# Two mixture-of-experts layers behind a random-feature attention: batch 0's sums of squares on ScalarE and VectorE, omega's low part from PSUM, late constants behind a maximum, gate matrices side by side

## The chip, the core and the metric

The kernel runs on one core of a Trainium2 chip. The engines are TensorE (PE, with its weight loads PEld), VectorE (DVE), ScalarE (ACT), GpSimd (POOL) and SyncE (SP, which issues most transfers). Each engine works through its own queue in order and waits at an instruction until what it needs is there. The metric is the device time of one execution in microseconds; a kernel is run several times and the median counts.

## What is computed

The reference is a chain of three steps on 2 batches of 576 tokens, 8 heads of 64.

```python
def phi(x):                                   # x: q or k, scaled by 64**-0.25
    h = einsum('bhsd,md->bhsm', x, omega)     # omega: 128 x 64
    h = h - sum(x * x, axis=-1) / 2
    return exp(h - max(h)) / sqrt(128)
kv, z = einsum(k_p, v), sum(k_p)              # per head, over all tokens
attn = (q_p @ kv) / (q_p . z + 1e-6)          # 1152 x 512 after the heads are joined

logits = attn @ w_gate                        # 8 experts, top 1 of a token
y = p(top1) * sigmoid(attn @ w_output_gate)[top1] * relu(attn @ w1[e]) @ w2[e]

out = sum over 4 experts of probs[:, e] * relu(y @ dw1[e]) @ dw2[e]
```

All in float32. The kernel writes each operand of a large product as a high part (rounded to the float32r format) and a low part (the rest), and takes high x high, high x low and low x high.

## The kernel before

The attention goes first and takes about the first 130 us. A group is one batch and half of the heads (four): `(b, hh)`. A group has 4 x 128 tokens of its own; the 64 tokens left over of both batches are kept together as `kr`, `vr`, `qr` (called the rest). The loop at the end of `moe_stack`'s attention part runs over `banks`, in the order k of a group, then q of it: 4 banks each (two token blocks `jp`, two head pairs `hp`), plus one bank of the rest for each half of the heads in batch 0. For a bank the steps are:

- `squares`, once for a group's k or q and for the rest: sum over 64 of x*x into `sq`, which the bias of the exponential needs. Before the change the first group's k goes on VectorE (a product and a reduction for each of its four transfers) and the eight others on GpSimd, as one product and six halving additions.
- `stage_a`: four transposes on PE into a PSUM tile `pt`, then the scaled copy `qTh` on ScalarE and the low part `qTl` on VectorE.
- `stage_b`: three products per half bank with omega's high part `omh` and low part `oml` into `pj`; on VectorE the maximum `mx`, then two small instructions with `sq` that give the bias `nb`; on ScalarE four exponentials `e`.
- `stage_ck` (k) adds to `kv` in PSUM; `stage_cq` (q) transposes `e`; `stage_d` multiplies with `kvs`, divides on VectorE, transposes and writes the high part `xh` (ScalarE) and the low part `xl` (VectorE) of the attention's output.

When a batch is through, `gate` takes the gate logits (`gate_logits`, `gate_tr`), and `main_expert` finds the expert that most tokens of the batch chose; SP reads its number and loads its weights. The products of the first expert layer (`ph`) are already mixed into batch 1's attention. Behind that come the layers of the two mixtures, which take the other 500 us.

What an engine does next is set by the order in which a scheduler in the compiler laid out the instructions; the queues hold that order at run time. `prep_late` makes constants that the gates need (`fold`, `cmask`, `iota` and others, and the high and low parts of the gate matrices) and the second mixture's probabilities `pb`. It is called at step `LATE`, but the scheduler may move its instructions up to where their inputs are there. Omega's high part is copied out of a float32 copy `omT`, its low part is `omT` less `omh`. The `WARM` products `wu` at the start use only constants.

Of the kernel before, what the change touches and what calls it, by code (L numbers as in the profile page):

```python
# [9 lines left out]
F32 = mybir.dt.float32  # L10
F32R = mybir.dt.float32r
# [10 lines left out]
M = 128  # L22
# [2 lines left out]
KB, FB = DM // 128, FF // 128  # L25
NC = 288
NX = B * S
WARM = 8
LATE = 12
HBUFS = 4  # L30
GROUPS = ((0, 320), (640, 256))
# [7 lines left out]
def moe_stack(ctx, tc, q, k, v, omega, w_gate, w_ogate, mw1, mw2, dprobs, dw1, dw2, out):  # L39
# [3 lines left out]
    def f32(ap):  # L43
        return ap.bitcast(F32)
# [34 lines left out]
    rev = cp.tile([128, NE], F32, name="rev")  # L79
    ue = cp.tile([128, 4, NE], F32, name="ue")  # L80
    uc = cp.tile([128, 4, NE], F32, name="uc")
    lgr = cp.tile([16, 128], F32, name="lgr")
    cnt = cp.tile([128, 4, NE], F32, name="cnt")
    ohb = cp.tile([128, 2, NE], F32, name="ohb")
    pb = cp.tile([128, 9, NE2], F32, name="pb")
# [88 lines left out]
        nc.sync.dma_start(dpr[64 * b:64 * b + 64, 8, :], dprobs[S * b + 512:S * b + 576])  # L174


    omT = cp.tile([128, 2, M], F32, name="omT")
    nc.vector.memset(omT, 0.0)
    pt = ps_t.tile([128, 4, 128], F32, tag="pt", name="pt")
    nc.tensor.transpose(pt[:, 0, :], om2.rearrange("p r d -> p (r d)"), ident)  # L180
    for r in range(2):
        nc.scalar.copy(omT[64 * r:64 * r + 64, r, :], pt[64 * r:64 * r + 64, 0, :])
    omh = cp.tile([128, 2, M], F32R, name="omh")
    oml = cp.tile([128, 2, M], F32R, name="oml")
    nc.scalar.copy(omh, omT)
    TT(oml, omT, f32(omh), op=ALU.subtract)
    wgh = cp.tile([128, KB, 16], F32R, name="wgh")
    wgl = cp.tile([128, KB, 16], F32R, name="wgl")

    def prep_late():  # L190
        TT(fold, ident[:, 0:32], ident[:, 32:64], op=ALU.add)
        TT(fold, fold, ident[:, 64:96], op=ALU.add)
        TT(fold, fold, ident[:, 96:128], op=ALU.add)
        nc.vector.tensor_reduce(cmask, ident.rearrange("p (c r) -> p c r", r=32), axis=AX.X, op=ALU.add)
        nc.gpsimd.iota(i32, pattern=[[1, 32]], base=0, channel_multiplier=0)
        nc.vector.tensor_copy(iota, i32)
        TS(iota1, iota, 1.0, None, op0=ALU.add)
        TS(rev, iota[:, 0:NE], -1.0, float(NE), op0=ALU.mult, op1=ALU.add)
        nc.vector.tensor_copy(ue, iota[:, 0:NE].unsqueeze(1).to_broadcast([128, 4, NE]))
        nc.vector.tensor_copy(uc, iota[:, 0:4].unsqueeze(2).to_broadcast([128, 4, NE]))  # L200
        nc.vector.memset(lgr, 0.0)
        split(wgh, wgl, wg)
        ds_ = cp.tile([128, 9], F32, name="ds_")
        nc.vector.tensor_reduce(ds_, dpr, axis=AX.X, op=ALU.add)
        TS(ds_, ds_, 1e-9, None, op0=ALU.add)
        nc.vector.reciprocal(ds_, ds_)
        TT(pb, dpr, ds_.unsqueeze(2).to_broadcast([128, 9, NE2]), op=ALU.mult)
# [3 lines left out]
    def squares(kind, b, hh, eng):  # L211

        src = raw[kind, b, hh] if b < 2 else raw[kind, 2]
        x = src.rearrange("p h j d -> p (h j) d") if b < 2 else src
        n = x.shape[1]
        x2 = ap.tile([128, n, D], F32, tag="x2", name="x2")
        s = ap.tile([128, n], F32, tag="sq" + kind + ("r" if b == 2 else ""), name="sq")
        if eng is nc.vector:
            for h in range(0, n, 4):
                TT(x2[:, h:h + 4], x[:, h:h + 4], x[:, h:h + 4], op=ALU.mult)  # L220
                nc.vector.tensor_reduce(s[:, h:h + 4], x2[:, h:h + 4], axis=AX.X, op=ALU.add)
        else:
            nc.gpsimd.tensor_tensor(x2, x, x, op=ALU.mult)
            w = D // 2
            while w:
                dst = x2[:, :, 0:w] if w > 1 else s.unsqueeze(2)
                nc.gpsimd.tensor_tensor(dst, x2[:, :, 0:w], x2[:, :, w:2 * w], op=ALU.add)  # L227
                w //= 2
        sq[kind, b, hh] = s

    def stage_a(kind, b, hh, jp):

        rest = b == 2
        src = raw[kind, b, hh] if not rest else raw[kind, 2]
        n = 2 if rest else G
        ps = ps_t.tile([128, G, 128], F32, tag="pt", name="pt")
        t, tl = (ap.tile([128, G, 128], F32R, tag=g, name=g) for g in ("qTh", "qTl"))
        for i in range(n):
            blk = src[:, i, 2 * jp:2 * jp + 2, :] if not rest else src[:, G * hh + 2 * i:G * hh + 2 * i + 2, :]
            nc.tensor.transpose(ps[:, i, :], blk.rearrange("p a d -> p (a d)"), ident)  # L240
        nc.scalar.activation(t[:, :n], ps[:, :n], AF.Copy, scale=SCALE)
        STT(tl[:, :n], ps[:, :n], SCALE, f32(t[:, :n]), op0=ALU.mult, op1=ALU.subtract)
        st_a[kind, b, hh, jp] = t, tl

    flip = [0]

    def stage_b(kind, b, hh, jp, hp):

        rest = b == 2
        t, tl = st_a[kind, b, hh, jp]  # L250
        if rest:
            s = sq[kind, 2, 0][:, G * hh:G * hh + G].rearrange("p (a c) -> p a c", a=2)
        else:
            s = sq[kind, b, hh].rearrange("p (h j) -> p h j", j=4)[:, 2 * hp:2 * hp + 2, 2 * jp:2 * jp + 2]
        e = ap.tile([128, 2, 2, M], F32, tag="e" if not rest else f"er{kind}{hh}", name="e", bufs=EB if not rest else 1)
        ps = ps_j.tile([128, 2, 2, M], F32, tag="pj", name="pj")
        for i in range(2):
            x = 2 * hp + i
            nc.tensor.matmul(ps[:, i], t[:, x], omh, start=True, stop=False)
            nc.tensor.matmul(ps[:, i], t[:, x], oml, start=False, stop=False)  # L260
            nc.tensor.matmul(ps[:, i], tl[:, x], omh, start=False, stop=True)
        mx = ap.tile([128, 2, 2], F32, tag="mx", name="mx", bufs=4)
        nc.vector.tensor_reduce(mx, ps, axis=AX.X, op=ALU.max)

        nb = ap.tile([128, 2, 2], F32, tag="nb", name="nb", bufs=4)
        hs = SCALE * SCALE / 2
        STT(mx, s, -hs, mx, op0=ALU.mult, op1=ALU.add)
        STT(nb, s, -hs, mx, op0=ALU.mult, op1=ALU.subtract)
        flip[0] += 1
        if flip[0] % FLIP:  # L270
# [88 lines left out]


    def gate_logits(b, psp, tag):
        lgs = cp.tile([16, 4, 128], F32, tag="lgs", name="lgs")
        for c in range(2):
            ps = psp.tile([16, NC], F32, tag=tag, name="lgp")
            cc = 2 * b + c
            mms = []
            for kb in range(KB):
                for a, x in ((wgh, xh), (wgh, xl), (wgl, xh)):
                    mms.append((a[:, kb, :], x[:, kb, NC * cc:NC * cc + NC]))
            for i, (a, x) in enumerate(mms):  # L370
                nc.tensor.matmul(ps, a, x, start=i == 0, stop=i == len(mms) - 1)
            nc.scalar.copy(lgs[:, 2 * c:2 * c + 2, :], ps[:, 0:256].rearrange("p (t n) -> p t n", n=128))
            nc.vector.tensor_copy(lgr[:, 32 * cc:32 * cc + 32], ps[:, 256:NC])
        return lgs

    def gate_tr(b, lgs, psp, tag):
        ps = psp.tile([128, 5, 16], F32, tag=tag, name="lgt")
        for t in range(5):
            nc.tensor.transpose(ps[:, t, :], lgs[:, t, :] if t < 4 else lgr, ident[:16, :16])
        lg = cp.tile([128, 5, 16], F32, tag=f"lg{b}", name="lg")  # L380
        nc.vector.tensor_copy(lg, ps)
        return lg
# [130 lines left out]
    for st in range(n + LAGD + 2):  # L513
        if st < n:
            kind, b, hh, jp, hp = banks[st]
            if b < 2 and jp == 0 and hp == 0:
                squares(kind, b, hh, nc.vector if (kind, b, hh) == ("k", 0, 0) else nc.gpsimd)
                if kind == "k" and (b, hh) != (0, 0):
                    i = 2 * b + hh + 1
                    if i < 4:  # L520
                        load_group(i // 2, i % 2)
            if b == 2 and hh == 0:
                squares(kind, 2, 0, nc.gpsimd)
            if st == LATE:
                prep_late()
            if hp == 0:
                stage_a(kind, b, hh, jp)
        if 1 <= st <= n:
            stage_b(*banks[st - 1])
        if 0 <= st - 1 - LAG < n:  # L530
            for u in tiles_of(banks[st - 1 - LAG]):
                do_c(u)
        if 0 <= st - 1 - LAGD < n:
            for u in tiles_of(banks[st - 1 - LAGD]):
                do_d(u)
# [389 lines left out]
```

## Time and profile before

| | |
|---|---|
| time of 3 runs | 638.55, 641.35, 645.41 us; median 641.35 |
| the profiled execution | 640.9 us, span 638.5 us, granted clock 0.997 |
| busy in the span | PE 614.5 us (96%), DVE 437.9 (69%), ACT 263.2 (41%), POOL 265.3 (42%) |
| the chain of waits that ended last | PE 84%, DVE 8%, POOL 3% of the span |

Busy time of PE is not PE at its peak: a product that lies in the queue behind another is counted from its start, so that a full stretch reads 100% and a slower one may read 90%. The count of products in a stretch says more. A wait inside an instruction (for a port, say) shows as a longer instruction, not as idle time.

### The profile page before, as it was taken

How to read it: one execution, taken by the hardware profiler on the slowest of the kernel's cores; microseconds unless marked ns; L12 is line 12 of the kernel's file. 1: busy time of each engine (PE TensorE's matmuls, PEld its weight loads, DVE VectorE, ACT ScalarE, POOL GpSimd, SP SyncE). 2: the span in 40 equal slices, each digit the busy share in tenths (PEclk: the TensorE clock that was granted, in tenths of full speed). 3: DMA queues.
4: the chain of work that ended last, by engine and by line, in shares of the span. 5: the costliest groups of instructions: out<-in, count | busy, mean ns of one | idle time of the engine just before them, and what ended most of it. 6: DMA issues, size and time to landing. Idle time of an engine off the chain costs nothing.

```text
span 638.5 us, 10737 instructions
## 1 busy us (share of the span) xinstructions
PE 614.5 (96%) x3985; PEld 564.1 (88%) x3986; DVE 437.9 (69%) x947; ACT 263.2 (41%) x630; POOL 265.3 (42%) x303
## 2 busy tenths in 40 slices
PE   7899999989998999899999999999999999999997
PEld 6788898889998999689989899899899898898995
DVE  6898588885284568976766756756666667666564
ACT  4658575504062234534434433433433343343230
POOL 3994024700000001557537536646646645745220
PEclk9999999989999999999999999999999999999999
DMA  8621034005133302201201201102201102100004
GB/s 200 154 67 34 2 133 132 2 4 195 67 131 133 132 2 67 66 2 37 97 1 59 73 1 67 68 0 67 67 1 66 67 1 67 66 1 2 0 1 148
DMA packets 38180, 39.60 MB, mean 62 GB/s; under 512 B 14448, under 2 KB 26736, under 8 KB 38128
## 3 DMA queue, kind: packets, MB, share of 16 engines
q1 hardware_dynamic: 37840, 38.85, 19.5%
q8 instruction: 31, 0.51, 0.3%
q14 instruction: 21, 0.17, 0.1%
q10 hardware_dynamic: 288, 0.07, 0.0%
HBM read 36.55 MB, written 2.36 MB: 61 GB/s over the span
## 4 chain that ended last, share of the span: by engine, by line
PE 84%; DVE 8%; POOL 3%; issue 1%; SPq 1%; DMA 1%; ACT 1%; POOLq 0%; ACTq 0%
PE po L553 10%; PE po L552 10%; PE po L554 10%; PE pp L552 9%; PE pp L554 9%; PE pp L553 9%; PE py L552 3%; PE py L554 3%; PE py L553 3%; PE ph L553 3%; PE ph L552 3%; PE ph L554 3%; PE pnd L337 2%; POOL x L227 2%; PE kv L289 2%
## 5 line engine op out<-in xcount | busy, mean ns | idle before, releaser
L90 POOL TENSOR_TENSOR wlo<-st,whi 128x512 fp32r<-128x512 f32 x104 | 126.4, 1238 | 241.5 <-ACT whi L89 241.5
L89 ACT CAST whi<-st 128x512 fp32r<-128x512 f32 x144 | 81.8, 596 | 141.4 <-PE po L554 51.9
L874 DVE SCALAR_TENSOR_TENSOR oacc<-po,pb,oacc 128x512 f32<-128x512 f32 x135 | 100.1, 749 | 56.0 <-PE po L554 56.0
L554 PE MATMUL po<-whi,hl 128*128 128x512 f32 x288 | 112.1, 390 | 0.7 <-POOL hl L548 0.6
L552 PE MATMUL po<-whi,hh 128*128 128x512 f32 x288 | 112.5, 391 | 0.0
L553 PE MATMUL po<-wlo,hh 128*128 128x512 f32 x288 | 112.4, 390 | 0.0
L548 POOL TENSOR_TENSOR hl<-c,hh 128x320 fp32r<-128x320 f32 (+1 forms) x64 | 53.2, 831 | 89.1 <-ACT hh L547 76.5
L552 PE MATMUL pp<-xh,whi 128*128 128x320 f32 (+1 forms) x256 | 75.8, 297 | 0.4 <-DVE u L833 0.2
L554 PE MATMUL pp<-xh,wlo 128*128 128x320 f32 (+1 forms) x256 | 75.7, 296 | 0.0
L553 PE MATMUL pp<-xl,whi 128*128 128x320 f32 (+1 forms) x256 | 75.7, 296 | 0.0
L554 PEld LDWEIGHTS po<-whi,hl 128*128 128x128 f32 x288 | 54.0, 188 | 12.9 <-POOL hl L548 1.0
L552 PEld LDWEIGHTS po<-whi,hh 128*128 128x128 f32 x288 | 54.1, 188 | 10.6 <-ACT hh L542 0.2
L553 PEld LDWEIGHTS po<-wlo,hh 128*128 128x128 f32 x288 | 54.1, 188 | 10.0
L821 DVE TENSOR_TENSOR c<-u,pp 128x320 f32<-128x320 f32 (+1 forms) x96 | 43.2, 453 | 21.7 <-PE pp L554 21.2
L546 ACT ACTIVATE c<-c 128x320 f32<-128x320 f32 (+1 forms) x64 | 28.5, 445 | 54.4 <-DVE c L821 53.7
L552 PEld LDWEIGHTS pp<-xh,whi 128*128 128x128 f32 x256 | 48.4, 190 | 2.3 <-DVE u L839 0.6
L553 PEld LDWEIGHTS pp<-xl,whi 128*128 128x128 f32 x256 | 48.5, 190 | 1.2
L552 PE MATMUL ph<-xh,whi 128*128 128x288 f32 (+1 forms) x160 | 47.9, 299 | 1.7 <-issue 1.7
L552 PE MATMUL py<-hh,whi 128*128 128x288 f32 x160 | 49.1, 307 | 0.0
L554 PEld LDWEIGHTS pp<-xh,wlo 128*128 128x128 f32 x256 | 48.5, 190 | 0.0
L553 PE MATMUL ph<-xl,whi 128*128 128x288 f32 (+1 forms) x160 | 48.0, 300 | 0.0
L543 DVE SCALAR_TENSOR_TENSOR hl<-c,hh 128x320 fp32r<-128x320 f32 (+1 forms) x64 | 45.9, 751 | 3.0 <-ACT hh L542 3.0
(217 smaller groups left out, 1424.5 us busy)
## 6 DMA issues: line engine op xcount, KB each, us to landing
st<-in_moe_w_dram SPq DMA_DIRECT2D x32, 512.0 KB, 4.1
st<-in_moe_w_dram SPq DMA_DIRECT2D x12, 1024.0 KB, 5.4
v<-in_v_dram SPq DMA_DIRECT2D x16, 128.0 KB, 3.9
q<-in_q_dram SPq DMA_DIRECT2D x4, 512.0 KB, 5.2
out_dram<-oacc SPq DMA_DIRECT2D x8, 256.0 KB, 2.1
k<-in_k_dram SPq DMA_DIRECT2D x3, 512.0 KB, 5.1
k<-in_k_dram SPq DMA_DIRECT2D x4, 128.0 KB, 2.7
kr<-in_k_dram SPq DMA_DIRECT2D x2, 128.0 KB, 3.6
```

The source lines that it names most:

```text
L89: nc.scalar.copy(hi, src)
L90: eng.tensor_tensor(lo, src, f32(hi), op=ALU.subtract)
L227: nc.gpsimd.tensor_tensor(dst, x2[:, :, 0:w], x2[:, :, w:2 * w], op=ALU.add)
L289: nc.tensor.matmul(kvps[key][:, i, :], e[i][r0:r1], v65[i], start=first and i == 0, stop=last and i == G - 1)
L543: STT(hl, src, 0.0, f32(hh), op0=ALU.max, op1=ALU.subtract)
L546: nc.scalar.activation(c, c, AF.Relu)
L548: nc.gpsimd.tensor_tensor(hl, c, f32(hh), op=ALU.subtract)
L552: nc.tensor.matmul(ps, sh_, mh, start=start, stop=False)
L553: nc.tensor.matmul(ps, sh_, ml, start=False, stop=False)
L554: nc.tensor.matmul(ps, sl_, mh, start=False, stop=stop)
L821: TT(c, u, p, op=op)
L874: STT(oacc[:, T], po, pc, oacc[:, T], op0=ALU.mult, op1=ALU.add)
```

## The change

`squares` with `nc.vector` now takes the products on ScalarE (`AF.Square`) and the reduction over 64 on VectorE; all of batch 0 and of the rest go there (six calls, five of which were on GpSimd), and batch 1's four stay on GpSimd. The first group's k is reduced in four pieces, its transposes are copied and corrected in halves. Omega's high part is copied from PSUM into a zeroed tile, the low part is PSUM less that; `omT` is gone. `prep_late` is issued behind the maximum of the bank before it. The gate matrices' high and low parts lie side by side in `wgs` with 32 columns, so that a block of the gate logits takes two products and not three, and `fold2` adds the two halves in the products that took the place of the transposes. `WARM` goes from 8 to 6.

```diff
-WARM = 8
+WARM = 6
...
-    omT = cp.tile([128, 2, M], F32, name="omT")
-    nc.vector.memset(omT, 0.0)
+    omh = cp.tile([128, 2, M], F32R, name="omh")
+    oml = cp.tile([128, 2, M], F32R, name="oml")
+    nc.vector.memset(f32(omh), 0.0)
+    nc.vector.memset(f32(oml), 0.0)
     pt = ps_t.tile([128, 4, 128], F32, tag="pt", name="pt")
     nc.tensor.transpose(pt[:, 0, :], om2.rearrange("p r d -> p (r d)"), ident)
     for r in range(2):
-        nc.scalar.copy(omT[64 * r:64 * r + 64, r, :], pt[64 * r:64 * r + 64, 0, :])
-    omh = cp.tile([128, 2, M], F32R, name="omh")
-    oml = cp.tile([128, 2, M], F32R, name="oml")
-    nc.scalar.copy(omh, omT)
-    TT(oml, omT, f32(omh), op=ALU.subtract)
-    wgh = cp.tile([128, KB, 16], F32R, name="wgh")
-    wgl = cp.tile([128, KB, 16], F32R, name="wgl")
+        rows = slice(64 * r, 64 * r + 64)
+        nc.scalar.copy(omh[rows, r, :], pt[rows, 0, :])
+        TT(oml[rows, r, :], pt[rows, 0, :], f32(omh[rows, r, :]), op=ALU.subtract)
+    wgs = cp.tile([128, KB, 32], F32R, name="wgs")
...
-        split(wgh, wgl, wg)
+        split(wgs[:, :, 0:16], wgs[:, :, 16:32], wg)
+        TT(fold2, ident[0:32, 0:16], ident[0:32, 16:32], op=ALU.add)
...
         if eng is nc.vector:
-            for h in range(0, n, 4):
-                TT(x2[:, h:h + 4], x[:, h:h + 4], x[:, h:h + 4], op=ALU.mult)
-                nc.vector.tensor_reduce(s[:, h:h + 4], x2[:, h:h + 4], axis=AX.X, op=ALU.add)
+            step = 4 if (b, hh) == (0, 0) and kind == "k" else n
+            for h in range(0, n, step):
+                nc.scalar.activation(x2[:, h:h + step], x[:, h:h + step], AF.Square)
+                nc.vector.tensor_reduce(s[:, h:h + step], x2[:, h:h + step], axis=AX.X, op=ALU.add)
...
-        nc.scalar.activation(t[:, :n], ps[:, :n], AF.Copy, scale=SCALE)
-        STT(tl[:, :n], ps[:, :n], SCALE, f32(t[:, :n]), op0=ALU.mult, op1=ALU.subtract)
+        step = 2 if (kind, b, hh) == ("k", 0, 0) else n
+        for i in range(0, n, step):
+            part = slice(i, i + step)
+            nc.scalar.activation(t[:, part], ps[:, part], AF.Copy, scale=SCALE)
+            STT(tl[:, part], ps[:, part], SCALE, f32(t[:, part]), op0=ALU.mult, op1=ALU.subtract)
...
-        nc.vector.tensor_reduce(mx, ps, axis=AX.X, op=ALU.max)
+        behind[0] = nc.vector.tensor_reduce(mx, ps, axis=AX.X, op=ALU.max)
...
-                for a, x in ((wgh, xh), (wgh, xl), (wgl, xh)):
-                    mms.append((a[:, kb, :], x[:, kb, NC * cc:NC * cc + NC]))
+                for x in (xh, xl):
+                    mms.append((wgs[:, kb, :], x[:, kb, NC * cc:NC * cc + NC]))
...
-            nc.tensor.transpose(ps[:, t, :], lgs[:, t, :] if t < 4 else lgr, ident[:16, :16])
+            nc.tensor.matmul(ps[:, t, :], lgs[:, t, :] if t < 4 else lgr, fold2, start=t == 0, stop=t == 4)
...
-                squares(kind, b, hh, nc.vector if (kind, b, hh) == ("k", 0, 0) else nc.gpsimd)
+                squares(kind, b, hh, nc.vector if b == 0 else nc.gpsimd)
...
-                squares(kind, 2, 0, nc.gpsimd)
+                squares(kind, 2, 0, nc.vector)
             if st == LATE:
-                prep_late()
+                with tc.issue_after(behind[0].ins):
+                    prep_late()
```

How the change moves instructions is read from the queues' order. The line numbers are each kernel's own: up to L178 they agree, and L220 to L379 of before are L222 to L384 of the change.

ScalarE's queue from its start, of before (`om` is omega as loaded, `pt` its transpose or that of k, `e` the exponentials of the first k banks):

```order
L57 ACT_TABLE_LOAD
L165 DMA om_120<-in_omega_dram 128x64 x2
L182 COPY omT<-pt 64x128 x2
L185 CAST omh<-omT 128x256
L241 ACTIVATE qTh<-pt 128x512 x2
L241 ACTIVATE qTh<-pt 128x256
L275 ACTIVATE e<-pj,nb 128x128 x16
L241 ACTIVATE qTh<-pt 128x512
L275 ACTIVATE e<-pj,nb 128x128 x4
```

The same of the change (`x_174`, `x_257`, `x_285` are the squares of the first group's k, of the rest's k `kr`, and of the first group's q):

```order
L57 ACT_TABLE_LOAD
L166 DMA om_119<-in_omega_dram 128x64 x2
L222 ACTIVATE x_174<-k_122 128x256 x4
L222 ACTIVATE x_257<-kr 128x512
L186 CAST omh<-pt 64x128 x2
L246 ACTIVATE qTh<-pt 128x256 x4
L280 ACTIVATE e<-pj,nb 128x128 x4
L246 ACTIVATE qTh<-pt 128x256
L280 ACTIVATE e<-pj,nb 128x128 x12
L222 ACTIVATE x_285<-q_140 128x1024
L246 ACTIVATE qTh<-pt 128x512
```

The squares of `kr` now stand ahead of omega's copy `omh`, and the squares of the first q ahead of the copies of its transposes.

VectorE's queue, of before, behind the first reductions (`iota`, `fold`, `cmask`, `rev`, `ue`, `uc` are late constants):

```order
L221 TENSOR_REDUCE sq<-x_176 128x4
L196 CAST iota<-i_104 128x32
L191 TENSOR_TENSOR fold<-ident 128x32
L194 TENSOR_REDUCE cmask<-ident 128x4
L192 TENSOR_TENSOR fold<-fold,ident 128x32
L197 TENSOR_SCALAR iota_106<-iota 128x32
L198 TENSOR_SCALAR rev<-iota 128x8
L193 TENSOR_TENSOR fold<-fold,ident 128x32
L199 COPY ue<-iota 128x32
L200 COPY uc<-iota 128x32
L186 TENSOR_TENSOR oml<-omT,omh 128x256
L242 SCALAR_TENSOR_TENSOR qTl<-pt,qTh 128x512 x2
```

The same place of the change:

```order
L223 TENSOR_REDUCE sq<-x_174 128x4 x4
L223 TENSOR_REDUCE sq<-x_257 128x8
L187 TENSOR_TENSOR oml<-pt,omh 64x128 x2
L247 SCALAR_TENSOR_TENSOR qTl<-pt,qTh 128x256 x2
L268 TENSOR_REDUCE mx<-pj 128x4
L247 SCALAR_TENSOR_TENSOR qTl<-pt,qTh 128x256
L272 SCALAR_TENSOR_TENSOR mx<-sq,mx 128x4
```

The late constants no longer stand ahead of `oml`; the reduction of `kr`'s squares does.

VectorE's queue of the change where the late constants went (`x_660` are the squares of the second group's q):

```order
L223 TENSOR_REDUCE sq<-x_660 128x16
L268 TENSOR_REDUCE mx<-pj 128x4
L191 TENSOR_TENSOR fold<-ident 128x32
L194 TENSOR_REDUCE cmask<-ident 128x4
L272 SCALAR_TENSOR_TENSOR mx<-sq,mx 128x4
L192 TENSOR_TENSOR fold<-fold,ident 128x32
L196 CAST iota<-i_102 128x32
L273 SCALAR_TENSOR_TENSOR nb<-sq,mx 128x4
L193 TENSOR_TENSOR fold<-fold,ident 128x32
L197 TENSOR_SCALAR iota_104<-iota 128x32
L198 TENSOR_SCALAR rev<-iota 128x8
L199 COPY ue<-iota 128x32
```

They now lie between the maxima and the small instructions of a later bank, behind the last of the five reductions that came over from GpSimd.

## Rows read from the trace of the kernel before

**Rows 1.** Stretches of 10 us: busy us and instructions by engine, clock, DMA.

```profile
core 0: us, PE busy (x) PEld busy (x) DVE busy (x) ACT busy (x) POOL busy (x), PEclk, DMA share, GB/s
10.00:20.00 10.00, 8.86 (x72) 8.23 (x72) 7.06 (x18) 6.62 (x23) 6.00 (x12) 1.00 0.99 235
20.00:30.00 10.00, 8.19 (x61) 6.89 (x60) 9.55 (x18) 6.09 (x21) 9.12 (x17) 1.00 0.72 163
...
40.00:50.00 10.00, 9.46 (x77) 8.47 (x76) 9.89 (x24) 6.13 (x21) 9.69 (x15) 1.00 0.23 65
...
60.00:70.00 10.00, 9.96 (x89) 9.76 (x89) 7.24 (x27) 6.47 (x20) 0.00 (x0) 1.00 0.00 0
70.00:80.00 10.00, 10.00 (x84) 8.36 (x83) 5.38 (x20) 5.58 (x19) 0.00 (x0) 1.00 0.01 2
```

**Rows 2.** Chain of waits that ended last: start us, us, what.

```profile
14.42 1.90 POOL x L223
...
23.65 1.85 POOL x L223
...
29.20 1.86 POOL x L223
...
33.47 0.59 DVE qTl L242
```

**Rows 3.** Groups by line and shape, DVE, 0 to 60 us: busy us, mean ns.

```profile
L263 DVE TENSOR_REDUCE mx<-pj 128x4 f32<-128x512 f32 x22 | 14.9, 682 | 4.6 <-PE pj L261 4.6
L267 DVE SCALAR_TENSOR_TENSOR mx<-sq,mx 128x4 f32<-128x4 f32 x22 | 10.2, 469 | 0.2
L268 DVE SCALAR_TENSOR_TENSOR nb<-sq,mx 128x4 f32<-128x4 f32 x21 | 7.7, 371 | 0.2
...
L221 DVE TENSOR_REDUCE sq<-x 128x4 f32<-128x256 f32 x4 | 1.6, 415 | 0.1
```

**Rows 4.** Timeline, 22 to 33 us: start us, us of all, engine, line, count.

```profile
22.37 0.15 DVE L268 SCALAR_TENSOR_TENSOR nb<-sq,mx 128x4 f32<-128x4 f32 x1
...
23.32 1.13 ACT L275 ACTIVATE e<-pj,nb 128x128 f32<-128x128 f32 x4
...
29.16 1.89 POOL L223 TENSOR_TENSOR x<-q 128x1024 f32<-128x1024 f32 x1
29.45 1.62 DVE L267 SCALAR_TENSOR_TENSOR mx<-sq,mx 128x4 f32<-128x4 f32 x1
...
31.13 3.37 POOL L227 TENSOR_TENSOR x<-x 128x512 f32<-128x512 f32 x5
...
32.54 0.18 DVE L204 TENSOR_REDUCE ds__528<-dpr 128x9 f32<-128x36 f32 x1
```

**Rows 5.** Chain of waits, the first batch's gate logits.

```profile
74.96 2.24 PE lgp L371 x17
```

**Rows 6.** Timeline of the start: start us, us, engine, line [idle before].

```profile
7.07 1.19 POOL L223 TENSOR_TENSOR x<-kr 128x512 f32<-128x512 f32 x1 [5.55 <-DMA kr<-in_k_dram]
...
7.23 1.06 DVE L199 COPY ue<-iota 128x32 f32<-128x32 f32 x1
...
8.29 0.41 DVE L186 TENSOR_TENSOR oml<-omT,omh 128x256 fp32r<-128x256 f32 x1
...
8.76 0.39 PE L260 MATMUL pj<-oml,qTh 128*128 128x256 f32 x1 [2.02 <-DVE oml L186]
...
10.14 1.29 DVE L263 TENSOR_REDUCE mx<-pj 128x4 f32<-128x512 f32 x2 [0.23 <-PE pj L261]
```

**Rows 7.** Groups by line and shape, ACT, 0 to 60 us.

```profile
L241 ACT ACTIVATE qTh<-pt 128x512 fp32r<-128x512 f32 x10 | 6.0, 609 | 0.0
L241 ACT ACTIVATE qTh<-pt 128x256 fp32r<-128x256 f32 x4 | 1.6, 388 | 5.9 <-PE pt L240 5.9
```

**Rows 8.** Stretches of 2 us in and behind TensorE's one slow spell.

```profile
132.00:134.00 2.00, 2.00 (x11) 2.00 (x10) 1.79 (x11) 0.31 (x1) 0.00 (x0) 0.53 0.00 0
134.00:136.00 2.00, 2.00 (x18) 2.00 (x17) 0.99 (x2) 0.00 (x0) 0.00 (x0) 1.00 0.00 0
```

More of the change, by code (lines that the diff above doesn't have):

```diff
@@ L81, in moe_stack @@
     uc = cp.tile([128, 4, NE], F32, name="uc")
-    lgr = cp.tile([16, 128], F32, name="lgr")
+    lgr = cp.tile([32, 128], F32, name="lgr")
+    fold2 = cp.tile([32, 16], F32, name="fold2")
     cnt = cp.tile([128, 4, NE], F32, name="cnt")
@@ L240, in stage_a @@
             nc.tensor.transpose(ps[:, i, :], blk.rearrange("p a d -> p (a d)"), ident)
-        nc.scalar.activation(t[:, :n], ps[:, :n], AF.Copy, scale=SCALE)
-        STT(tl[:, :n], ps[:, :n], SCALE, f32(t[:, :n]), op0=ALU.mult, op1=ALU.subtract)
+        step = 2 if (kind, b, hh) == ("k", 0, 0) else n
[3 more added lines that the diff above has]
+            STT(tl[:, part], ps[:, part], SCALE, f32(t[:, part]), op0=ALU.mult, op1=ALU.subtract)
         st_a[kind, b, hh, jp] = t, tl
-    flip = [0]
+    flip, behind = [0], [None]
     def stage_b(kind, b, hh, jp, hp):
@@ L361, in gate_logits @@
     def gate_logits(b, psp, tag):
-        lgs = cp.tile([16, 4, 128], F32, tag="lgs", name="lgs")
+        lgs = cp.tile([32, 4, 128], F32, tag="lgs", name="lgs")
         for c in range(2):
-            ps = psp.tile([16, NC], F32, tag=tag, name="lgp")
+            ps = psp.tile([32, NC], F32, tag=tag, name="lgp")
             cc = 2 * b + c
```

## The prediction, made before the changed kernel ran

> **What bounds the kernel now.** I read the stretches of 10 us first, for where TensorE falls short. A full stretch issues 84 to 89 products (60 to 80 us); from 10 to 30 us it is 72 and 61, and 77 from 40 to 50 [rows 1]. So there is slack in about the first 50 us, and behind them PE has no room: what the change takes off the early stretch should move the rest forward unchanged, and what it takes off PE later counts in full. The same rows name two suspects for the early slack: VectorE at 9.55 and 9.89 of 10, GpSimd at 9.12 and 9.69. ScalarE is idle for nearly 4 of 10 us.
>
> The chain of waits says how they hang together. From 14.42 to about 33 us it runs through GpSimd alone, one sum of squares behind the other, and leaves it for VectorE at 33.47 [rows 2]. Two neighbouring products of a whole group start 5.55 us apart (23.65, 29.20); the q of the first group and the rest's q together fill 14.42 to 23.65, so that a rest takes 3.7. The other thing to see is the length of the two small instructions that use the sums: 469 and 371 ns on average [rows 3], where a free one takes 0.15 us; one that starts 0.29 us behind a GpSimd product ends with it, 1.62 us later [rows 4]. VectorE's 9.9 of 10 is thus partly waiting: (10.2 - 22 x 0.15) + (7.7 - 21 x 0.15) = 11.4 us in 43 instructions.
>
> **The change part by part.** The sum is made against the profiled execution, 640.9 us; the median of the runs is 641.35, so 0.45 is added at the end.
>
> *Gate logits.* 48 products become 32. 17 in a row take 2.24 us in the chain [rows 5], 0.132 each, so 16 fewer are 2.1 us, 1.05 per batch. Batch 0's lie in a full PE stretch [rows 1]. Bounds: 0 (if something else sets the end there) and 2.1; I take **-2.1**, as they stand in the chain itself. The transposes become products of the same count; the two rows of `fold2` and the wider copy I cost at nothing, beside ScalarE's idle time.
>
> *Start.* Before, the second product waited 2.02 us for `oml` (8.29), which stood behind the late constants, among them 1.06 us of `ue` that GpSimd's product on `kr` held up [rows 6]. The constants go, but ScalarE's queue now has the square of `kr` ahead of `omh`, and VectorE's has its reduction ahead of `oml`. `kr` is there at 7.07, when GpSimd starts on it [rows 6]. A square of 512 columns I price as the scaled copy of that width, 0.61 us [rows 7]: `omh` begins at 7.7, the first copy of k ends by about 8.5, `oml` follows the reduction (0.68, as a maximum of 512 columns [rows 3]) at 8.4 to 8.8. The first bank's maximum, at 10.14 before, comes at about 9.7. Nearly all that the constants gave up is eaten by `kr`. The shorter warm-up is worth nothing, as PE waits there anyway. Bounds: -2.0 (the wait goes whole) and +1.0.
>
> *VectorE's balance from 8 to 50 us.* Off come the port waits of five of nine GpSimd calls. By GpSimd time, batch 0 is 3 x 5.55 + 2 x 3.7 = 24.0 us and batch 1 4 x 5.55 = 22.2, so 52% of 11.4: -6.0. On come reductions: 0.415 us for 256 columns and 0.682 for 512 [rows 3] give 1.21 for 1024; three of these and one of 512 are +4.3 (that of `kr` lies in the wait for data). Late constants: eleven small ones that ran ahead of `oml`, 0.15 to 0.18 us each [rows 4], 0.1 where they overlap (two maxima of 0.682 take 1.29 [rows 6]): +1.1. Net **-0.6**.
>
> *VectorE's idle time.* From 10 to 30 us it is 2.94 + 0.45 = 3.4 us [rows 1]. A new wait comes: the square of the first q stands behind all 16 exponentials of k on ScalarE. These take 1.13 us for four [rows 4], start at about 11.7 and end at 16.3; the square of 1024 columns (0.61 + 2 x 0.22, by the step from 256 to 512 [rows 7]) ends at 17.4, while VectorE has run out of k work at about 15.5. That is 1.9 us idle, 2.4 with small waits. **-1.0**.
>
> *Where the chain goes.* From 17.4: the reduction to 18.6, two low parts of q and two maxima of 0.68 to 21.4, and one more maximum before the bias: q's first exponentials at 22.2 against 23.32 [rows 4]. The next two banks gain the waits of the long small instructions too, so that at 28 us I count about 2.5 us. Some is lost again: batch 1's squares stay on GpSimd and start as soon as their data is there instead of at 29.2 + 5.55 = 34.7 [rows 2], since the queue is free, and hold VectorE at that time. I take **-2.0** for the attention in all (-0.6, -1.0 and -0.4 of the start). Bounds: -6 (the first rival) and +1.
>
> One rule bears on the reductions. A VectorE reduction beside a running GpSimd addition (31.13 to 34.5) took 0.18 us at 32.54, not held up, while the instruction with two inputs in SBUF was [rows 4]. That is what I price by. *The Trainium skill, SBUF — State Buffer, section "Who interferes with whom", says that VectorE and GpSimd share one port pair under an exclusive lock, that an instruction with two SBUF inputs or a two-port mode blocks on it, and that a reduction on trn2 never does; the trace agrees for this one reduction (0.18 us).* Without this, the last of the moved reductions, which meets batch 1's first product, could be held up to 1.89 us more [rows 4].
>
> Sum: -2.1 - 2.0 = -4.1, 636.8 on the profiled execution, 637.2 against the median: **637 us**, with 634 to 639.5 for this case alone.
>
> **The rivals.**
>
> *Nothing takes GpSimd's place (25%).* With the chain through GpSimd gone [rows 2], PE may come near the rate of 60 to 70 us: in 10 to 30 us it is 17 + 28 products short of 89 [rows 1], 5.1 us. With the gates that is 640.9 - 7.2 = 633.7, **634**. For it: ScalarE has 7.3 us idle in these 20. Against: VectorE's net relief is 0.6 us.
>
> *Late constants collide (13%).* They now stand among the small instructions of a later bank, at some 26 to 31 us by the count above, when batch 1's first squares may run. GpSimd held VectorE for 11.4 of its 46 us, a quarter; eleven dense small instructions in 5.55 us could make it half to all, +1.4 to +4. The attention's gain is gone: 640.9 - 2.1, **639**.
>
> *TensorE's clock (7%).* The granted clock fell to 0.53 (of 2.4 GHz, so its 1.2 GHz level) only once, behind PE's waits for the gates: 11 products in 2 us, against 18 behind it [rows 8], 0.07 us more each. Now PE does less at the start and idles longer until about 8.4. *The Trainium skill, TensorE: Matmul & The Clock Gate, Part 1, says that the array's default is the lower level and that activity releases it; that speaks against the shorter warm-up.* If the 30 projections of the first k ran at the lower level, that is +2.1, partly beside VectorE: **639**. Before, the wait of 2.02 us at 8.76 did not bring it down.
>
> *ScalarE's queue becomes the bound, slower than before (10%).* Each square stands in order ahead of copies and exponentials that PE and VectorE wait for, and each waits for a transfer. The four later squares are 3 x 1.05 + 0.61 = 3.8 us; if each falls on the path, and omega's copies with the first k (up to 2), the end moves 5.8 - 2.1 later, **644.6**. It decides if q's first exponentials come later than 24.5 us. Against: the 7.3 us of idle time, and the copies of q had no need to be early.
>
> **How the numbers follow.** The forecast has 45%. For 8 in 10 the range goes from 632 (most of the first rival) to 642 (the forecast, the collisions and the clock, with half of the bounds above); the slower rival is left out. About 1% is what a measurement of this kernel can tell: faster means below 634.9, slower above 647.8. Faster: the first rival's 25% and the lower edge of the forecast's, 0.30. Slower: the last rival's upper part, 0.06. Same: 0.64.
>
> **What would show it.** In the profile after: 32 products of gate logits at 0.13 us, and the chain no longer through GpSimd before 25 us. `omh` behind `kr`'s square at about 7.7 and the first maximum near 9.7. A wait of VectorE for ScalarE's square of q at 15.5 to 17.4, q's first exponentials near 22.2. Small instructions of 0.15 us until batch 1's first square starts on GpSimd, and long ones from there. PE's count from 20 to 30 us above 61, by less than 28. The prediction is wrong if the count stays (the gain is the gates' alone) or if the last of batch 0's products comes over 5 us earlier, or if the clock of the first 20 us is below 1.

## The result, and the profile after

The changed kernel takes 649.45 us (median of 4 runs, 648.03 to 650.79), the kernel before 641.07 beside it: ratio 1.0137, 95% interval 1.0097 to 1.0177 (the ratios leave out executions over 1.5% above the fastest of the same kernel). It is slower by about 8.4 us, where 637 was forecast and 642 was the range's end. The profiled execution has a span of 648.6 us, 10.1 more than before, and a mean granted clock of 0.981 against 0.997.

Where the time went is read first from the stretches of 10 us of the changed kernel, in the columns of [rows 1]:

```profile
10.00:20.00 10.00, 9.85 (x73) 9.48 (x72) 7.05 (x20) 7.28 (x24) 0.00 (x0) 1.00 1.09 243
20.00:30.00 10.00, 7.28 (x55) 6.43 (x55) 8.66 (x20) 7.98 (x22) 3.05 (x3) 1.00 0.70 159
30.00:40.00 10.00, 6.41 (x45) 5.59 (x43) 10.00 (x19) 4.29 (x14) 9.45 (x12) 0.85 0.20 52
40.00:50.00 10.00, 8.83 (x43) 8.83 (x43) 6.76 (x24) 2.95 (x8) 2.37 (x8) 0.50 0.01 2
60.00:70.00 10.00, 9.99 (x72) 9.42 (x71) 7.68 (x24) 8.04 (x28) 1.34 (x5) 0.83 0.15 34
```

Counted from the start and without the warm-up, TensorE has issued 146 products at 30 us before and 134 after; at 50 us 290 and 220; at 100 us 690 and 612. At 8.5 a microsecond (170 from 60 to 80 us before) that is 1.4, 8.2 and 9.2 us behind. At 28 us the two are level (129 each). So the loss falls between 28 and 50 us, most of it behind 30 us, with VectorE at 10.00 of 10 and only 19 instructions from 30 to 40 us, and hardly changes behind it. From 20 to 30 us the count is 55, where the prediction looked for more than 61.

The timeline of that place, of the changed kernel (start us, us, engine, line; in brackets the idle time before it and what ended it):

```profile
31.00 1.21 DVE L223 TENSOR_REDUCE sq<-x 128x16 f32<-128x1024 f32 x1
32.56 1.89 POOL L225 TENSOR_TENSOR x<-q 128x1024 f32<-128x1024 f32 x1
32.73 1.77 DVE L191 TENSOR_TENSOR fold<-ident 128x32 f32<-128x32 f32 x1
34.42 0.27 DVE L194 TENSOR_REDUCE cmask<-ident 128x4 f32<-128x128 f32 x1
34.62 1.19 DVE L272 SCALAR_TENSOR_TENSOR mx<-sq,mx 128x4 f32<-128x4 f32 x1
35.91 0.68 DVE L273 SCALAR_TENSOR_TENSOR nb<-sq,mx 128x4 f32<-128x4 f32 x1
36.54 1.92 POOL L225 TENSOR_TENSOR x<-k 128x1024 f32<-128x1024 f32 x1
36.62 1.87 DVE L197 TENSOR_SCALAR iota<-iota 128x32 f32<-128x32 f32 x1
36.63 1.14 ACT L280 ACTIVATE e<-pj,nb 128x128 f32<-128x128 f32 x4 [3.12 <-DVE nb L273]
39.07 1.14 DVE L91 TENSOR_TENSOR wgs<-wg,wgs 128x64 fp32r<-128x64 f32 x1
40.35 0.17 DVE L205 TENSOR_REDUCE ds__511<-dpr 128x9 f32<-128x36 f32 x1
```

`fold` (1.77 us) and `iota` (1.87) each start just behind a GpSimd product and end with it, where their like took 0.15 to 0.18 before [rows 4]; the bias instructions `mx` (1.19) and `nb` (0.68) and the split `wgs` (1.14) lie beside its additions and are held as well. From `fold` (32.73) to `ds` (40.35) the queue takes 7.62 us. ScalarE waits 3.12 us for the bias `nb` that stands in this queue, then TensorE has little to do (8 products in the 4 us behind 36), and its clock falls. The same stretch in steps of 2 us:

```profile
34.00:36.00 2.00, 0.94 (x8) 0.73 (x7) 2.00 (x6) 0.00 (x0) 1.84 (x3) 1.00 0.48 170
36.00:38.00 2.00, 0.90 (x4) 0.94 (x5) 2.00 (x3) 1.14 (x4) 2.00 (x2) 0.74 0.00 0
38.00:40.00 2.00, 0.79 (x4) 0.49 (x3) 2.00 (x6) 0.00 (x0) 2.00 (x3) 0.50 0.00 0
48.00:50.00 2.00, 2.00 (x12) 2.00 (x11) 1.40 (x4) 0.84 (x2) 0.00 (x0) 0.50 0.00 0
50.00:52.00 2.00, 2.00 (x17) 2.00 (x16) 1.37 (x7) 1.44 (x6) 0.21 (x1) 0.85 0.00 0
```

From 38 to 50 us the clock is at 0.50 (1.2 GHz). TensorE has work again from 42 us, and gets 11 or 12 products through in 2 us where [rows 8] show 18 at the full clock. The stall is paid twice: once as idle time, once in the work behind it, some 3 us here (6 products fewer in each of four steps). *The Trainium skill, TensorE: Matmul & The Clock Gate, section "HAM oscillation — how this bites in real kernels", says of a kernel that waits for a transfer in every round that such a wait brings the clock down again, so that the work behind it starts at the lower level; the trace agrees, here behind waits for VectorE (0.50 from 38 to 50 us).*

The start, of the changed kernel, against [rows 6]:

```profile
7.24 0.24 ACT L186 CAST omh<-pt 64x128 fp32r<-64x128 f32 x1
7.97 0.27 DVE L187 TENSOR_TENSOR oml<-pt,omh 64x128 fp32r<-64x128 f32 x1
9.00 0.45 PE L242 MATMUL pt<-ident,k 128*128 128x128 f32 x1 [3.56 <-DVE oml L187]
9.68 0.41 PE L266 MATMUL pj<-omh,qTl 128*128 128x256 f32 x1
9.89 0.41 PE L264 MATMUL pj<-omh,qTh 128*128 128x256 f32 x1
10.77 0.69 DVE L268 TENSOR_REDUCE mx<-pj 128x4 f32<-128x512 f32 x1 [0.50 <-PE pj L266]
24.55 3.21 ACT L280 ACTIVATE e<-pj,nb 128x128 f32<-128x128 f32 x12 [0.26 <-DVE nb L273]
```

Omega's parts come about when forecast, but TensorE stands still for 3.56 us, and its first projections follow each other at 0.21 us. The first maximum is at 10.77, not 9.7; q's first exponentials are at 24.55, not 22.2. This profile gives the clock as 1.00 from 8 to 14 us. That of e3 below, with the same start, gives 0.50 there at the same count (11 products from 10 to 12 us in both), so the lower level is likely here too, but this trace does not record it.

### The profile page after: what moved, and what is told of

Its sections match the earlier page's. It is cut to its first block, busy times and chain, and to the rows that moved or that the text cites. A ratio compares the mean times of both kernels' runs of the same rounds, so it can differ in the third digit from the quotient of the medians.

```text
span 648.6 us, 10702 instructions
## 1 busy us (share of the span) xinstructions
PE 620.2 (96%) x3975; PEld 573.5 (88%) x3976; DVE 436.9 (67%) x953; ACT 268.1 (41%) x640; POOL 243.1 (37%) x268
## 4 chain that ended last, share of the span: by engine, by line
PE 88%; DVE 8%; ACT 1%; issue 1%; POOL 1%; DMA 0%; SPq 0%; DVEq 0%; POOLq 0%; ACTq 0%
PE po L559 10%; PE po L558 10%; PE po L560 10%; PE pp L558 9%; PE pp L560 8%; PE pp L559 8%; PE py L558 3%; PE ph L558 3%; PE ph L559 3%; PE ph L560 3%; PE py L560 3%; PE py L559 3%; PE kv L294 3%; PE pnd L342 2%; PE pj L264 1%; PE pj L266 1%
## 5 line engine op out<-in xcount | busy, mean ns | idle before, releaser
L560 PE MATMUL ph<-xh,wlo 128*128 128x288 f32 (+1 forms) x160 | 48.5, 303 | 0.0
```

Source lines behind the costliest of these rows:

```text
L560: nc.tensor.matmul(ps, sl_, mh, start=False, stop=stop)
```

## The experiments

All ratios are to the kernel before, run on the same chip beside the experiment, with a 95% interval.

**The late constants and GpSimd's squares, a table of two by two.** Theory A: the constants, dense and behind a maximum, meet batch 1's squares on GpSimd. Its rival: the start (clock and order) made the loss.

```diff
 e1_free (the changed kernel with)     e3_nopool (the changed kernel with)
-  with tc.issue_after(behind[0].ins): -  squares(kind, b, hh, nc.vector if b == 0 else nc.gpsimd)
-      prep_late()                     +  squares(kind, b, hh, nc.vector)
+  prep_late()                         e13_both: both edits
```

> The changed kernel, with the late constants no longer issued behind a maximum. Theory A (the late constants, put among batch 1's GpSimd squares, are held up one by one, PE starves and its clock falls): the loss goes, about 639 us, no stretch of low clock from 37 to 51 us. Theory B (the squares on ScalarE stand ahead of omega's copy and of exponentials): stays at 647 to 650 us. Theory C (the shorter warm-up leaves the first projections at the lower clock, and that carries on): stays at 647 to 650 us.

> The changed kernel, with batch 1's four sums of squares on ScalarE and VectorE as well, so that GpSimd runs none while the late constants stay behind the maximum. Theory A: 634 to 638 us, small instructions of 0.15 us throughout. Theory B: slower still, 650 to 654 us, since four more squares of 1.05 us and four reductions of 1.21 us come on. Theory C: 648 us.

> The changed kernel with both suspects taken away: batch 1's squares on ScalarE as batch 0's are, so that GpSimd squares nothing, and the late constants free to be issued where the scheduler puts them. With the changed kernel (649.45), e1_free (645.01) and e3_nopool (641.69) it makes a table of two by two. Theory A (the constants' place costs time because GpSimd's squares lengthen small VectorE instructions there): without GpSimd's squares their place is worth 1 us or less, so 640.5 to 642.5, with small VectorE instructions at 0.1 to 0.25 us between 28 and 48 us. Theory B (the wait behind the maximum costs by itself, whoever else works): the 4.4 us that e1_free gained are gained again, 636.5 to 638.5.

| changed kernel | constants behind a maximum | constants free |
|---|---|---|
| batch 1's squares on GpSimd | 649.45, 1.0137 (1.0097 to 1.0177) | e1: 645.01, 1.0052 (1.0021 to 1.0083) |
| batch 1's squares on ScalarE | e3: 641.69, 0.9999 (0.9967 to 1.0030) | e13: 640.40, 0.9973 (0.9941 to 1.0006) |

Freeing the constants is worth 0.85% beside GpSimd's squares and 0.26% without them (the intervals of e3 and e13 overlap); taking the squares off GpSimd is worth 1.4% and 0.8%. That is theory A's direction, but the times alone do not settle it: 0.85% less 0.26% is 0.6%, with an interval of some 0.7% to either side, and taking the squares off is worth 0.8% even with the constants free. e13 ends 0.1 us below its range, e1 won back less than was expected of it, and both e3's median and its profiled execution (638.68) lie above the 634 to 638 that were expected. What shows that GpSimd's squares stretch the constants is the length of the instructions. e3's timeline of the same constants, and its stretch of 10 us:

```profile
31.86 0.17 DVE L191 TENSOR_TENSOR fold<-ident 128x32 f32<-128x32 f32 x1
32.59 0.17 DVE L197 TENSOR_SCALAR iota<-iota 128x32 f32<-128x32 f32 x1
33.05 0.15 DVE L91 TENSOR_TENSOR wgs<-wg,wgs 128x64 fp32r<-128x64 f32 x1
33.21 0.17 DVE L205 TENSOR_REDUCE ds__511<-dpr 128x9 f32<-128x36 f32 x1
```

```profile
30.00:40.00 10.00, 10.00 (x91) 9.88 (x90) 9.31 (x40) 8.75 (x25) 0.00 (x0) 1.00 0.18 54
```

From `fold` to `ds` 1.35 us instead of 7.62, and 91 products in the stretch instead of 45. The lead does not last: e3 is 14 products ahead of before at 50 us and level with it at 100 us (690 each). Why e1 stays slower is in its timeline: most constants have gone, yet the instructions left there are still held.

```profile
33.73 1.52 DVE L206 TENSOR_SCALAR ds__511<-ds__511 128x9 f32<-128x9 f32 x1
37.39 1.85 DVE L272 SCALAR_TENSOR_TENSOR mx<-sq,mx 128x4 f32<-128x4 f32 x1
```

**One part alone, in the kernel before.** e2_behind adds only the place of the late constants; x1_squares adds only the squares of batch 0 and of the rest on ScalarE and VectorE.

```diff
 e2_behind                                x1_squares
-  prep_late()                          -  squares(..., nc.vector if (kind, b, hh) == ("k", 0, 0) else nc.gpsimd)
+  with tc.issue_after(behind[0].ins):  +  squares(..., nc.vector if b == 0 else nc.gpsimd)
+      prep_late()                      (the rest's likewise, with the product as AF.Square)
```

> The kernel before, with only the late constants issued behind the maximum. Theory A: slower, 645 us or more, since GpSimd squares run there as well. Theories B and C: 641 us, as before.

> The kernel before, with only batch 0's and the rest's squares on ScalarE and VectorE. Theory A (VectorE's instructions on SBUF are held up while GpSimd runs batch 1's squares, which now start at about 27 us, and TensorE's clock falls behind the stall): 642 to 645 us, like the run with the late constants free. Theory B (the five GpSimd calls gone are what counts, the rest of the change is the loss): 637 to 640 us.

e2: 649.91 (645.77 to 654.12, 4 runs), ratio 1.0163 (1.0088 to 1.0238). x1: 643.39, 1.0040 (1.0019 to 1.0061). The constants' place alone is enough for such a loss; the squares alone cost 2.6 us, where the prediction had the whole attention win 2. The parts don't add up (9.1 and 2.6 against 8.4 together): both lose at the same place. The clock has no part in x1's loss: its median is 0.995, before's 0.993. e2's stretches show the stall small and the clock behind it large:

```profile
30.00:40.00 10.00, 7.70 (x58) 6.81 (x57) 9.69 (x33) 5.18 (x17) 9.06 (x14) 0.97 0.17 55
40.00:50.00 10.00, 10.00 (x65) 10.00 (x65) 7.24 (x19) 3.89 (x13) 9.69 (x15) 0.69 0.18 53
```

But in e2 hardly anything holds the constants. They run beside GpSimd's additions, at 0.15 to 0.29 us each, and `fold` to `ds` take 2.14 us, among them the two bias instructions at 0.26 and 0.41. What is held behind them (1.47 us at 34.93) has its like before (`pb`, 1.82 us at 34.87). e2's timeline:

```profile
30.90 3.32 POOL L227 TENSOR_TENSOR x<-x 128x512 f32<-128x512 f32 x5
32.10 0.18 DVE L191 TENSOR_TENSOR fold<-ident 128x32 f32<-128x32 f32 x1
33.56 0.17 DVE L197 TENSOR_SCALAR iota<-iota 128x32 f32<-128x32 f32 x1
34.24 0.17 DVE L204 TENSOR_REDUCE ds__528<-dpr 128x9 f32<-128x36 f32 x1
```

TensorE is level with before at 28 us, 13 products behind at 40 and 24 at 50; its clock is at 0.50 from 40 to 46 us, though no single wait of it from 28 to 40 us is longer than 1.28 us. So held constants explain the 7.62 us of the changed kernel, but not e2's loss: some 2 us more in a queue that is busy for 9.69 of 10 us went with a loss of about the same size. Theory A's mechanism is not shown for e2, and the profiled execution (646.25 us) is one of its faster ones.

**An attempt that moved nothing.** x3_later issues batch 1's squares behind an older maximum, to move them away from the constants.

```diff
-  squares(kind, b, hh, nc.vector if b == 0 else nc.gpsimd)
+  if b == 0: squares(kind, b, hh, nc.vector)
+  else:
+      with tc.issue_after(maxima[-7]): squares(kind, b, hh, nc.gpsimd)
```

> The changed kernel, with batch 1's four GpSimd squares issued behind a maximum six or seven banks ahead of their use, so that the late constants meet no GpSimd work. Theory A: most of the loss goes, 640 to 643 us, the constants at 0.1 to 0.2 us each. Theory B' (the constants cost by their number and place alone): stays at 648 to 650 us.

651.07, ratio 1.0146 (1.0065 to 1.0226). The first of these squares starts at 27.34 us, against 27.00 in the changed kernel, and for the same reason:

```profile
27.34 1.89 POOL L225 TENSOR_TENSOR x<-k 128x1024 f32<-128x1024 f32 x1 [6.54 <-DVE sq L223]
```

It waits for a buffer that a reduction frees, not for the maximum. So the expectation missed, and the run says nothing on theory A.

**The start.** x4_warm14 is the changed kernel with `WARM = 14` instead of 6.

> The changed kernel with 14 warm-up products in place of 6, so that PE is busy until about 7 us. If the first projections' low pace (0.21 us each until 13 us) is of the loss: full pace (0.12) from the first, q's first exponentials 1 us earlier, 647 to 648.5 us. If the later stalls hide it: 649.5 us.

649.32, ratio 1.0123 (1.0090 to 1.0157): no gain at the end. The start did change; of x4:

```profile
9.65 0.28 PE L266 MATMUL pj<-omh,qTl 128*128 128x256 f32 x1
9.77 0.28 PE L264 MATMUL pj<-omh,qTh 128*128 128x256 f32 x1
```

0.12 us a projection instead of 0.21, and the third maximum at 12.59 instead of 13.77. The stall from 32 us on ate it: x4 is 6 products ahead of the changed kernel at 30 us and level at 40. y1_combo puts it where nothing eats it: e3 with `WARM = 14` and the rest's squares behind a maximum.

> The changed kernel with no sums of squares on GpSimd, 14 warm-up products, and the rest's squares behind a maximum. By theory A and the clock: faster than before, 634 to 638 us with the first projections at full pace; the fall of the clock behind the second gates stays. If ScalarE's and VectorE's added work binds: 642 us.

637.89, ratio 0.9944 (0.9913 to 0.9975), 3.8 us below e3 at the median, with intervals that overlap a little; which of the two edits did it was not taken apart.

**The gate.** e7_gate is the kernel before with the gate matrices side by side only.

> The kernel before, with only the gate matrices side by side (32 products for 48). All theories: 2.1 us less than before, 639 us; if the gates are not on the path, 641 us.

641.89, ratio 1.0045 (1.0011 to 1.0079): nothing of the 2.1 us. Its timeline at the second gates:

```profile
115.35 2.38 DVE L583 TENSOR_SCALAR dg<-ident,sel 128x128 f32<-128x128 f32 x2
115.50 1.26 POOL L91 TENSOR_TENSOR wlo<-st,whi 128x512 fp32r<-128x512 f32 x1
116.77 0.99 DVE L584 TENSOR_SCALAR dg<-fold,sel 128x32 f32<-128x32 f32 x1
117.67 0.26 DVE L374 COPY lgr<-lgp 32x32 f32<-32x32 f32 x2
117.89 0.61 PE L380 MATMUL lgt<-fold,lgs 32*128 32x16 f32 x4 [2.24 <-DVE lgr L374]
```

I took the VectorE instructions in this queue off it one kind after the other: `lgr`'s copy to ScalarE (e7b_lgr; y3_lgr from y1), the products `dg` of the gate rows as well (e7c_rows; y4_rows).

```diff
-  nc.vector.tensor_copy(lgr[...], ps[:, 256:NC])                  # e7b, y3
+  nc.scalar.copy(lgr[...], ps[:, 256:NC])
-  TS(dg[...], ident, s[:, t:t + 1], None, op0=ALU.mult)           # e7c, y4 as well
+  nc.scalar.activation(dg[...], ident, AF.Relu, scale=s[:, t:t + 1])
```

> The kernel before with the gate matrices side by side, and the copy of the last tile's logits (lgr) on ScalarE instead of VectorE. In e7_gate TensorE stood still for 2.24 us ahead of lgt, until VectorE had copied lgr, which was queued behind gate-row products of 1.40, 2.38 and 0.99 us beside GpSimd's weight splits; then its clock was 0.50 for 6 us. Theory A (that queue ate the gate's gain of 2.1 us): the gap before lgt falls to 1 us or less and the time to 637 to 640, 2 to 4.5 us below e7_gate's 641.89. Theory B (the shorter logits are worth nothing since experts wait for something else there, and the clock falls in any case): 641 to 643.

> y1_combo with the same edit: lgr's copy on ScalarE. In y1_combo TensorE stood still from 112.3 to 115.74 us, until VectorE had copied lgr behind products of 1.27, 1.87 and 1.23 us beside GpSimd, and its clock was 0.50 from 116 to 126 us. Theory A: the gap of 3.4 us shrinks to under 1 us, and if the clock stays up, up to 4 us more come back: 631 to 636. Theory B (other work than the copy sets the pace, or the clock falls in the new place as well): 637 to 639.

> y3_lgr with the gate rows' products (dg) on ScalarE instead of VectorE; the order of TensorE, GpSimd and SyncE is unchanged. In y3_lgr the 3.4 us gap ahead of lgt was gone, and a gap of 3.83 us stood ahead of the next step, the counts (cps): VectorE copied the logits (lg) at 118.89 only after products of 1.87, 1.25, 1.37 and 0.23 us beside GpSimd; then the clock was 0.50 from 120 to 126 us. Theory A (these held products are the wait at the second gates): the gap ahead of cps falls to 1.5 us or less; 2 to 4 us less time, 632.5 to 635. Theory B (the gate's chain is hidden there, or ScalarE's queue takes the products' place): 636 to 638.5.

> e7b_lgr with the gate rows' products on ScalarE as well, that is the kernel before with the gate matrices side by side, and both lgr's copy and the products off VectorE. Theory A (the gate's 2.1 us were eaten by VectorE's queue of products beside GpSimd's weight splits): 636.5 to 639.5. Theory B (they are eaten whatever VectorE does, by the clock or by another wait): 641 to 644.

e7b 643.53, 1.0039 (1.0017 to 1.0060); e7c 644.05, 1.0046 (1.0027 to 1.0066): theory B twice, each time just above its range. y3 636.59, 0.9924 (0.9897 to 0.9951), and y4 635.22, 0.9905 (0.9887 to 0.9923), lie between the theories and too close to y1 and to each other to be told apart. The wait moved on each time. In y3 the gap ahead of `lgt` was gone, and this one had come:

```profile
118.89 0.23 DVE L386 COPY lg<-lgt 128x80 f32<-128x80 f32 x1
119.72 0.62 PE L399 MATMUL cps<-gm_eq,ones 128*128 128x40 f32 x2 [3.83 <-DVE gm_eq L397]
```

In y4 that one was gone, and the small instructions behind it were held in their turn:

```profile
118.96 5.04 POOL L91 TENSOR_TENSOR wlo<-st,whi 128x512 fp32r<-128x512 f32 x4
121.46 1.35 DVE L437 TENSOR_TENSOR gm_oh<-gm_w,gm_wm 128x40 f32<-128x40 f32 x1
122.86 1.16 DVE L425 TENSOR_SCALAR ohb<-cb,cbm 128x8 f32<-128x8 f32 x1
```

So the last runs leave VectorE's queue as it is and take away what holds it: expert 0's 16 weight splits go from GpSimd to VectorE, with the gate in the kernel before (e7d_split), without it (e8_split, the control), and in y4 (y5_split). y6_free is y5 with the late constants free.

```diff
-  E0 = main_weights(0, nc.gpsimd)
+  E0 = main_weights(0, nc.vector)
```

> e7_gate (the kernel before with the gate matrices side by side, all else as it was) with expert 0's 16 weight splits on VectorE instead of GpSimd. Theory A (the gate's 2.1 us are eaten beside those splits): 637 to 639.8, with the gap ahead of lgt under 1 us. Theory B (they are eaten whatever VectorE does): 641 to 644.

> y4_rows with expert 0's 16 weight splits on VectorE instead of GpSimd. In y4_rows the gaps ahead of the transposes and the counts were gone, but between 114 and 124 us seven small VectorE instructions of the gate's chain took 1.13 to 1.35 us each beside those splits, and TensorE ran out of work at 124 to 128 us, with the clock at 0.50 for 5 us behind it. Theory A (GpSimd's splits hold the chain): every one of them at 0.1 to 0.3 us, the second gates 3 us earlier or more, against 16 x 0.6 us more on VectorE, part of it in its idle time: 631.5 to 634.5. Theory B (VectorE's added 10 us eat what it gains): 635 to 638.

> The kernel before with expert 0's 16 weight splits on VectorE instead of GpSimd, and nothing of the change: the control of e7d_split (635.25). Theory A (the gate's matrices side by side are worth 2.1 us where nothing eats them): 636.4 to 638.4. Theory B (the splits are worth all of e7d_split's 6.9 us, the gate nothing even so): 634.5 to 636.

> y5_split with the late constants free to be issued where the scheduler puts them, and not behind a maximum. Theory A (their place is worth about 1 us where GpSimd squares nothing, as e13_both against e3_nopool, 1.3 us): 630 to 631.5. Theory B (worth nothing here): 631 to 632.5.

| | us | ratio |
|---|---|---|
| e8_split: before, splits | 634.24 | 0.9868 (0.9829 to 0.9906) |
| e7d_split: before, splits, gate | 635.25 | 0.9896 (0.9863 to 0.9928) |
| y5_split: y4, splits | 631.50 | 0.9835 (0.9802 to 0.9868) |
| y6_free: y5, constants free | 631.17 | 0.9810 (0.9778 to 0.9843) |

That GpSimd's splits hold the second gates is shown: one word in the kernel before is worth 1.3%. At 100 us e8 is no further than before (702 products against 706, with the warm-up), at 140 us it is 44 ahead; `gm_eq` takes 0.19 us instead of 1.26, and TensorE's waits for VectorE between 100 and 150 us (4.0 us before) are gone. None of those waits was for a split weight, which speaks against the rival that the quicker splits bring the weights sooner. The edit also changes the order of VectorE's queue; what that does was not taken apart. In y5 the instructions shown for y4 are short:

```profile
121.62 0.19 DVE L437 TENSOR_TENSOR gm_oh<-gm_w,gm_wm 128x40 f32<-128x40 f32 x1
122.87 0.22 DVE L425 TENSOR_SCALAR ohb<-cb,cbm 128x8 f32<-128x8 f32 x1
```

From 120 to 140 us e8 issues 150 products where before has 116. e7d gained more than its theory A, and e8 says why: the splits make all of it. e8 and e7d, without and with the gate, are not told apart; so nothing of the gate's 2.1 us is seen even here, and theory A for e8 fell. What eats most of it is on TensorE itself, in one execution of each: its busy time (the first column) with the products of the logits (`lgp`, first line) and of what follows them (`lgt`, second line), 60 to 140 us, before first and then e7d:

```profile
60.00:140.00 80.00, 7.35 (x48) 4.30 (x48) 1.40 (x4) 1.44 (x4) 0.98 0.16 54
60.00:140.00 80.00, 1.63 (x10) 1.05 (x10) 0.47 (x2) 0.98 0.16 54
```

```profile
60.00:140.00 80.00, 5.29 (x32) 3.39 (x32) 0.70 (x4) 1.41 (x4) 1.00 0.16 54
60.00:140.00 80.00, 3.23 (x20) 2.65 (x20) 0.48 (x2) 1.00 0.16 54
```

16 products less take 2.06 us off; the ten transposes have become products with `fold2`, which run as 20, and put 1.60 back. That leaves 0.46 us, too little to see in these runs.

y5 and y6 beat both kernels; y6 against y5 is open (their intervals overlap).

## Why the prediction was wrong, point by point

- *VectorE's balance, the late constants (+1.1).* This is the step that failed. It priced eleven instructions at 0.1 us, as if they stood where nobody else works, while the next paragraph but one had batch 1's squares on GpSimd start early at the same time. `fold` to `ds` took 7.62 us, 1.35 without GpSimd's squares. What it allowed for these squares in the chain was half a us (2.5 down to 2.0). Nor was the place itself priced: e2, where the constants are hardly held and take 2.14 us, loses 9.1 us.
- *Late constants collide (13%, 639).* The place (32.7 us, where 26 to 31 were named) and, for the changed kernel, the mechanism were right, the size was not. The price of 1.4 to 4 us came from a share of GpSimd's time; the held instructions add up to 6.3 us more, and the rival had no term for the clock behind the stall. It also stood at too low a chance, since the forecast's own step put the squares there.
- *The clock.* It was weighed for the start alone. The 101 runs of the kernel before that the experiments' ratios use spread with it: a straight line through them is 638.0 us + 438 us x (1 - mean granted clock), with a scatter of 1.2 us. By this the medians' clocks, 0.993 and 0.982, go with 4.8 of the 8.4 us, which leaves 3.6 for the stall itself; for e2 (0.977) with 7.0 of 9.1. This is an estimate from one kernel's runs and a correlation: a wait lowers the clock and takes time of its own. It would explain why a stall of a few us costs 8.
- *Start (-0.4).* `omh` at 7.24 and `oml` from 7.97 were as forecast or earlier. "The shorter warm-up is worth nothing, as PE waits there anyway" was wrong: behind the wait the first projections ran at 0.21 us, and at 0.12 where TensorE was kept busy (x4). That x4's end didn't move shows it was hidden here, not that it was nothing.
- *Reductions and squares.* Nine calls were on GpSimd before, as the prediction has it (the description of the kernel says eight). The prices were right: 0.42, 0.69 and 1.21 us for the reductions, 0.63 and 1.07 for the squares on ScalarE, and the reduction at 31.00 took its 1.21 us beside a GpSimd addition. *The Trainium skill, SBUF — State Buffer, section "Who interferes with whom", says that a reduction never contends with GpSimd on this chip, while `tensor_scalar` can and a two-input instruction in SBUF does; the trace agrees: `cmask`, a reduction, 0.27 us (0.28 before, at a place without GpSimd's squares), `fold` 1.77 and `iota` 1.87.* I had used this for the reductions and not asked it of the constants.
- *VectorE's idle time and the chain (-1.0, -2.0).* The square of q started at 17.88 instead of 16.3 and q's exponentials at 24.55. VectorE's relief came (in x1 the waits inside the two bias instructions up to 60 us fell from 11.4 to 5.1 us, where 6.0 less were forecast), but no time followed from it: at 28 us before, the changed kernel, x1 and e3 are all level (129 products) instead of 2 to 2.5 us apart. At 30 us the changed kernel is 12 products behind before, x1 15, and e3, where GpSimd squares nothing, 10. So most of that step is not GpSimd's; the second q's square on ScalarE (1.16 us at 28.18) stands there, and the cause was not taken apart. By 40 us e3 is 8 ahead; x1 is 29 behind at 50.
- *Gate logits (-2.1).* The products were right (-2.06), "products of the same count ... at nothing" was not (+1.60), and in time nothing of the term came (e7 1.0045).
- *Nothing takes GpSimd's place (25%).* Not for this change, since batch 1's squares stayed there. Where they go too, it is what happens for a while (91 products from 30 to 40 us in e3), but the lead is gone at 100 us and the time is that of before.
- *ScalarE's queue (10%).* It had the direction, and its point of decision was just met (24.5; it was 24.55). But ScalarE waited for VectorE in the stall (3.12 us), and e3, with four more squares on ScalarE, is as fast as before, so ScalarE's queue was not the bound.

## What to carry to other kernels

A small VectorE instruction on SBUF has no fixed price: the same constants took 1.35 us, 2.14 us and 7.62 us here, by what GpSimd ran beside them (nothing, the short additions of a square, whole products). So ask of every group that is moved what GpSimd does at the new place, by the change's own schedule, and whether the queue has room there at all. Behind a stall that starves TensorE, add the work that then runs at the lower clock. If a wait moves on each time an instruction is taken out of a queue, take away what holds the queue.

## What the hardware showed that I had not expected

- Moving 16 weight splits of 512 columns from GpSimd (1.28 us) to the busier VectorE (0.68 us) made the kernel 1.3% faster: what GpSimd's copy of the work held up was worth more than VectorE's time.
- The ten products with `fold2`, in plain float32, ran as 20 of 0.26 us each; the transposes in whose place they stand ran as ten of 0.22.
- Without GpSimd's squares the two bias instructions take 151 and 153 ns on average from 0 to 60 us (e3), against 469 and 371 [rows 3].
